# DeltaNet and low-rank mixer: 32x32 blocks moved by VectorE transpositions, norms from gram diagonals, and two products formed ahead of the recurrence

## The chip, the cores and the metric

One core of one Trainium2 chip runs the whole kernel in one launch. The metric is device time in microseconds, the median of several executions. Five engines work side by side, each with its own instruction queue: TensorE (PE, matmuls; its weight loads are listed as PEld), VectorE (DVE), ScalarE (ACT), GpSimd (POOL) and SyncE (SP, which here only issues DMAs).

## What is computed

Two parts follow each other. The first is a delta-rule attention over a sequence of 768 tokens, for 4 batches of 8 heads with 48 dimensions:

```python
k_n = k / (np.linalg.norm(k, axis=-1, keepdims=True) + 1e-06)
for t in range(S):
    y[:, :, t] = q_t @ state
    v_old = state^T k_t
    state = state + beta_t * outer(k_t, v_t - v_old)
```

The second is a mixer on the heads laid side by side (x is 4 x 768 x 384):

```python
u = x + ((x^T @ U) @ V)^T           # U: 768 x 32, V: 32 x 768
out = u + max(u @ w_ch1, 0) @ w_ch2 # 384 -> 1536 -> 384
```

The weights arrive as 64-bit floats and are turned into 32-bit ones on the chip.

## The kernel before

**Tiles.** The sequence is cut into 12 chunks of 64 tokens. Six chunks of one batch, all heads, are a unit; there are 8 units (n = 0 to 7, two per batch), and they alternate between two slots of SBUF. Four pairs of heads (j, r) fill the partitions.

**A unit's preparation.** `norms` squares k on ScalarE (L315), sums on VectorE (L318), takes root and reciprocal, multiplies with beta (L333), and turns the result on TensorE (L342) into `cp`. `grams` transposes k and q on TensorE (L367), copies them out (L370, L373), and forms K K^T and K Q^T (L382), copied out on ScalarE (L393) or masked on VectorE (L397). `blocks` needs the inverse of a unit lower triangular 64x64 matrix per head and chunk. It inverts the 32x32 diagonal blocks by forward substitution with one block per partition. So each block has to move from "rows on partitions" to "one block on one partition" and back. For unit 0 that is done by TensorE with an identity (L465, L522), for the others by DMAs through a scratch tensor in DRAM, issued from SP (L479 and L486 there, L544 and L549 back). The substitution is a chain of pairs of VectorE instructions (L497, L503): 31 pairs for a block of 32, or 15 pairs where the block is first split into two of 16 (`split == 2`, units 0 and 1), which are then joined by small matmuls (L579, L598). `joins` also combines the two 32-blocks into the 64-block (L621, L638), `diagonals` copies blocks on GpSimd (L658) and clears others (L664). The result is called zt below, the Z of the title.

**The recurrence** (`recur`) runs chunk after chunk through a batch: B = K S (L704), rhs = v - B on VectorE (L725), C = Z rhs (L734), a copy z on ScalarE (L743), the new state's product (L749), the state's sum on VectorE (L772). The output is q S (L715) plus a product with z (L759), copied to X by ScalarE (L685).

**The mixer.** `load_weights` brings 27 slices by GpSimd's DMA queue (L818) into two buffers, and converts each with five VectorE instructions (L834, L843, L849, L854, L862) and one on ScalarE (L839). `sums` adds slices of w_ch2 on GpSimd (L798), because the second layer is computed with 7 products in place of 8. `front` forms u and its transpose for 256 tokens (L885, L899, L903, L907, L910), `wide` the two layers for these 256 tokens: 72 matmul records of L972, then 84 of L1005, with GpSimd sums between them (L944, L951). There are 12 such steps, 3 per batch. A 32-bit matmul shows as two records.

**The order.** The program's order is made by a planner inside the kernel (`run`): every part is a generator that yields operations with an estimated cost, an engine, a PSUM buffer to take or give and keys to wait for, and each part has a place, the lower the sooner: recurrence of batch 0 at 1, the fronts at 2, preparation of units 0 and 1 at 10 and 14, weights at 21 to 40, recurrences of the other batches at 59, preparation of later units from 68, the wide steps at 95. The planner's result is the order on each engine's queue, and it is not changed at run time. PSUM has eight banks: three pairs (banks 0-1, 2-3, 6-7) and two single ones (4, 5); pair 6-7 is handed to `wide` when its first step begins.

Of the kernel before, what the change touches and what calls it, by code (L numbers as in the profile page):

```python
# [8 lines left out]
FP32 = mybir.dt.float32  # L9
# [6 lines left out]
L = 64  # L16
BK = 32
# [9 lines left out]
def kernel(  # L27
# [51 lines left out]
    BANK = dict(pair=[0, 2, 6], one=[4, 5], mix=[6, 7])  # L79
# [4 lines left out]
    state = dict(now=0.0, mode=None, hw=0.0, slow=1.9)  # L84
    free = dict(pair={0: 0.0, 1: 0.0, 2: 0.0}, one={0: 0.0, 1: 0.0}, mix={})
    done, parts, waits, ready, last = {}, {}, {}, {}, {}
    LAT = dict(pe=0.22, dve=0.06, act=0.06, pool=0.1, sp=0.0)
    SWITCH, HOLD = 0.15, 0.15

# [6 lines left out]
    def op(engine, cost, mode=None, take=None, give=(), lat=None, rush=False):  # L96
        return dict(e=engine, cost=cost, mode=mode, take=take, give=give,
                    rush=rush or bool(give), lat=LAT[engine] if lat is None else lat)
# [7 lines left out]
    def landing(packets, each=0.015):  # L106
        state["hw"] = max(state["hw"], state["now"]) + packets * each / 16
        return max(1.9, state["hw"] + 1.4 - state["now"])
# [16 lines left out]
    def run():  # L125
        while waits:
# [23 lines left out]
            for e, them in some.items():  # L150
                soon = min(at for at, _ in them)
                them.sort(key=lambda x: (not waits[x[1]]["rush"], x[1]))
                for at, i in them:
                    hold = HOLD if i[0] < 90 else SWITCH
                    if at > soon + hold:
                        continue
                    if not any(a < at and a + waits[x]["cost"] < at + 0.05 for a, x in them):
                        picks.append((at, i))
                        break
# [6 lines left out]
            cost = s["cost"] * (state["slow"] if s["mode"] in ("F", "Q", "T") else 1.0)  # L166
# [11 lines left out]
    def one(x):  # L178
        return P[:, BANK["one"][x]]

# [23 lines left out]
    def views(slot):  # L204
# [6 lines left out]
        ksq = slot[:, 6144 : 6144 + CS * D].rearrange("p (c s d) -> p c s d", c=UC, s=4)  # L211
        kz = slot[:, 9216 : 9216 + 2 * UC * D].rearrange("p (c j d) -> p c j d", c=UC, j=2)
        return kn, kq, pg, qk, qn, vn, ksq, kz

    units = [views(slots[n % 2]) for n in range(N)]
    for i in range(2):
        nc.vector.memset(units[i][0][:, :, :, D:DP], 0.0)
        nc.vector.memset(units[i][4][:, :, :, D:DP], 0.0)

    upper_rows = const.tile([128, 1], FP32, name="upper_rows")  # L220
    nc.vector.memset(upper_rows, 0.0)
    for i in range(4):
        nc.vector.memset(upper_rows[quarter(i, SB)], -1.0)
    bias_e = const.tile([128, 1], FP32, name="bias_e")
# [6 lines left out]
    nc.vector.memset(P[:, 0:4], 0.0)  # L231
    nc.vector.memset(P[:, 4:8], 0.0)
    nc.vector.memset(gs, 0.0)
    cts = [const.tile([128, BK], FP32, name=f"ct{i}") for i in range(2)]
    for t in cts:
        nc.vector.memset(t, 0.0)
    betas = const.tile([128, B, NC, 4], FP32, name="betas")
# [8 lines left out]
    clock["dve"], clock["pool"] = 8.0, 2.5  # L246
# [4 lines left out]
    def load(n, name, halves):  # L251
# [3 lines left out]
        yield need(("rec", n - 2))  # L255
# [9 lines left out]
        for g in halves:  # L265
# [10 lines left out]
            emitted((name, n, g), after)  # L276
# [4 lines left out]
    def load_beta():  # L281
# [3 lines left out]
        for g in range(2):  # L285
            yield op("pool", 0.6)
            nc.gpsimd.dma_start(out=beta_sb[:, g], in_=beta[:, 4 * g : 4 * g + 4])
        yield op("pool", 0.0, lat=landing(64, 0.1))
        for u in range(NU):
            x = yield op("pe", 0.6, "Q", take="one")  # L290
            p_bt = one(x)[:, 0 : 4 * B * UC].rearrange("p (c x) -> p c x", c=UC)
            for cu in range(UC):
                c = UC * u + cu
                for g in range(2):
                    nc.tensor.matmul(
                        p_bt[half(g), cu], beta_sb[:, g, c * L : c * L + L],
                        ident[0 : 4 * B, 0 : 4 * B], start=True, stop=True,
                    )
            yield op("dve", dve(4 * B * UC), give=[("one", x)])
            nc.vector.tensor_copy(  # L300
                out=betas[:, :, UC * u : UC * u + UC].rearrange("p b c s -> p c b s"),
                in_=p_bt.rearrange("p c (b s) -> p c b s", s=4),
            )
            emitted(("betas", u), 0.1)
            yield need(("gram", u))

    def landed(name, n):
        return need(*[(name, n, g) for g in range(2)])

    def norms(n):  # L310
        kn, _, _, _, _, vn, ksq, _ = units[n]
        b, hf = divmod(n, NU)
        yield landed("k", n)
        yield op("act", act(CS * D))
        nc.scalar.square(ksq, kn[:, :, :, 0:D])  # L315
        yield op("dve", dve(CS * D))
        norm = small.tile([128, UC, 4], FP32, name="norm", bufs=3)
        nc.vector.tensor_reduce(out=norm, in_=ksq, axis=AX.X, op=ALU.add)  # L318
        emitted(("ksq", n), 0.1)
        yield op("act", 0.2)  # L320
        norm_k, norm = norm, small.tile([128, UC, 4], FP32, name="norm_v", bufs=3)
        nc.scalar.sqrt(
            norm.rearrange("p c (r j) -> p c j r", r=2),
            norm_k.rearrange("p c (j r) -> p c j r", r=2),
        )
        yield need(("betas", hf))
        yield op("dve", 1.1)
        nc.vector.tensor_scalar_add(norm, norm, 1e-6)
        rec = small.tile([128, UC, 4], FP32, name="rec")
        nc.vector.reciprocal(rec, norm)  # L330
        nc.vector.tensor_tensor(out=rec, in0=rec, in1=rec, op=ALU.mult)
        ct = cts[n % 2][:, 0:CS].rearrange("p (r c j) -> p r c j", r=2, c=UC)
        nc.vector.tensor_tensor(  # L333
            out=ct.rearrange("p r c j -> p c r j"),
            in0=rec.rearrange("p c (r j) -> p c r j", r=2),
            in1=betas[:, b, UC * hf : UC * hf + UC].rearrange("p c (j r) -> p c r j", r=2),
            op=ALU.mult,
        )
        x = yield op("pe", 0.1, "J", take="one")
        p_ct = one(x)[:, 0:BK]  # L340
        for i in range(4):
            nc.tensor.matmul(  # L342
                p_ct[quarter(i)],
                cts[n % 2][quarter(i)],
                ident[quarter(i), quarter(i)],
                start=True,
                stop=True,
            )
        yield op("act", act(BK), give=[("one", x)])
        nc.scalar.copy(cp[:, n % 2], p_ct)  # L350
        emitted(("c", n), 0.1)
# [3 lines left out]
            out=vn, in0=vn, in1=norm[:, :, :, None].to_broadcast([128, UC, 4, D]), op=ALU.mult  # L355
# [3 lines left out]
    def grams(n):  # L359
        kn, kq, pg, qk, qn, _, _, _ = units[n]  # L360

        def turn(t, c0, i):
            x = yield op("pe", 0.45, "F", take="one")
            p_t = one(x).rearrange("p (x j t) -> p x j t", x=2, j=2)
            for c in range(2):
                for j in range(2):
                    nc.tensor.transpose(p_t[:, c, j], t[:, c0 + c, 2 * j : 2 * j + 2].rearrange("p s d -> p (s d)"), ident)  # L367
            if n == 0 and i == 0:
                yield op("dve", dve(512), give=[("one", x)])
                nc.vector.tensor_copy(out=kq[:, c0 : c0 + 2, :, i], in_=p_t)  # L370
            else:
                yield op("act", act(512), give=[("one", x)])
                nc.scalar.copy(kq[:, c0 : c0 + 2, :, i], p_t)  # L373

        def products(c0, i):
            x = yield op("pe", 0.47, "Q", take="pair")
            p_g = pair(x)[:, :, 0:256].rearrange("p r (c j t) -> p r c j t", c=2, j=2)
            for c in range(2):
                for j in range(2):
                    for par, g in QUADS:  # L380
                        rows = half(par, D)
                        nc.tensor.matmul(  # L382
                            p_g[half(g ^ (par * i)), par, c, j],
                            kq[rows, c0 + c, j, 0, half(g)],
                            kq[rows, c0 + c, j, i, half(g)],
                            start=True,
                            stop=True,
                        )
            at = slice(c0, c0 + 2)
            to = pg[:, :, at].rearrange("p r c j t -> p r (c j t)")  # L390
            if i == 0:
                yield op("act", act(512), give=[("pair", x)])
                nc.scalar.copy(to, p_g.rearrange("p r c j t -> p r (c j t)"))  # L393
            else:
                for par in range(2):
                    yield op("dve", dve(256), give=[("pair", x)] if par else (), rush=True)
                    nc.vector.tensor_tensor(  # L397
                        out=qk[:, par, at].rearrange("p c j t -> p (c j) t"),
                        in0=p_g[:, par].rearrange("p c j t -> p (c j) t"),
                        in1=mask_u[:, None, :].to_broadcast([128, 4, L]),  # L400
                        op=ALU.mult,
                    )
            emitted(("product", n, c0, i), 0.1)

        for i, (name, t) in enumerate((("k", kn), ("q", qn))):
            for c0 in range(0, UC, 2):
                yield landed(name, n)
# [658 lines left out]
```

## Time and profile before

| | |
|---|---|
| median of 3 executions | 720.76 us (719.04 to 721.79) |
| profiled execution: its time / span | 725.51 us / 723.7 us |
| mean granted TensorE clock | 0.884 |
| TensorE busy | 637.3 us (88%), 10344 matmul records |
| VectorE busy | 377.1 us (52%), 925 instructions |
| ScalarE / GpSimd busy | 182.9 us / 215.0 us |
| scratch DMAs of the blocks | 4 kinds, 28 issues each, 96 KB each |

The span runs from the first instruction to the last, and 1.8 us lie around it. In the table by stretches used below, each row gives a stretch in us, its length, then busy time and number of instructions of PE, PEld, DVE, ACT and POOL, the granted clock of TensorE, the mean share of the DMA engines, and GB/s. In the timeline a row gives start and duration in us, engine, line, operation, out<-in, and in brackets the idle time before it with what ended it.

### The profile page before, as it was taken

The numbers are of one execution on the slowest core, as the hardware profiler recorded it, in microseconds if no ns is written. First come the engines' busy times: TensorE is split into PE (matmuls) and PEld (weight loads), VectorE is DVE, ScalarE is ACT, GpSimd is POOL, SyncE is SP. The second block draws the span as 40 slices with busy tenths as digits, with TensorE's granted clock in tenths as the row PEclk, the third lists the DMA queues.
The fourth block names the chain that finished last, engine by engine and source line by source line (L and its number), as shares of the span: only waits on it lengthen the run. The fifth ranks groups of instructions, "written<-read, shape, count | busy, mean of one in ns | idle before, by whom it ended". The sixth has DMA issues, their size and how long they took to land.

```text
span 723.7 us, 23375 instructions
## 1 busy us (share of the span) xinstructions
PE 637.3 (88%) x10344; PEld 540.5 (75%) x10344; DVE 377.1 (52%) x925; ACT 182.9 (25%) x399; POOL 215.0 (30%) x281
## 2 busy tenths in 40 slices
PE   5667688659598899999798999999799999999998
PEld 4556576528486688789686887798677887989997
DVE  7577768799958631249678240469494111201001
ACT  3232235325121241331112322421113112020110
POOL 7326341233450250130350511123604302231412
PEclk9965555559798999999979999999799799999999
DMA  9731439852060231342211321521402000000000
GB/s 155 126 92 28 120 84 184 183 125 67 0 122 24 45 73 36 74 88 56 54 36 34 74 56 39 109 48 36 90 24 45 3 24 2 23 0 23 1 23 22
DMA packets 132964, 44.27 MB, mean 61 GB/s; under 512 B 126336, under 2 KB 129408, under 8 KB 132864
## 3 DMA queue, kind: packets, MB, share of 16 engines
q1 hardware_dynamic: 127776, 30.20, 21.2%
q0 software_dynamic: 3488, 12.29, 6.5%
q8 instruction: 81, 1.33, 0.8%
q10 hardware_dynamic: 1600, 0.30, 0.3%
q14 instruction: 19, 0.16, 0.1%
HBM read 32.54 MB, written 10.22 MB: 59 GB/s over the span
## 4 chain that ended last, share of the span: by engine, by line
PE 52%; DVE 29%; DMA 8%; issue 4%; SPq 3%; ACT 1%; POOL 1%; ACTq 0%; DVEq 0%; POOLq 0%
PE P L1005 18%; PE P L972 16%; DVE prod L497 11%; DVE xt L503 10%; PE P L638 2%; PE P L621 2%; SPq L269 2%; PE P L382 2%; DMA slot<-in_q_dram 2%; PE P L899 2%; PE P L367 2%; PE P L734 2%; DMA scr<-xt 2%; DMA wide<-in_moe_w_ch_dram 1%; PE P L704 1%
## 5 line engine op out<-in xcount | busy, mean ns | idle before, releaser
L972 PE MATMUL P<-ut,w_sb 128*128 128x256 f32 x864 | 213.3, 396 | 0.0
L972 PEld LDWEIGHTS P<-ut,w_sb 128*128 128x128 f32 x864 | 161.8, 194 | 24.8 <-issue 0.6
L1005 PE MATMUL P<-w_sb,hs 128*128 128x192 f32 x720 | 129.5, 333 | 0.0
L1005 PEld LDWEIGHTS P<-w_sb,hs 128*128 128x128 f32 x720 | 118.3, 192 | 3.2
L944 POOL TENSOR_TENSOR S<-hs 128x384 f32<-128x384 f32 x24 | 24.7, 1030 | 256.6 <-ACT hs L928 256.6
L957 DVE TENSOR_TENSOR X<-X,P 128x192 f32<-128x192 f32 x84 | 29.5, 351 | 133.4 <-PE P L1005 133.2
L497 DVE TENSOR_TENSOR prod<-gs,xt 128x112 f32<-128x112 f32 (+21 forms) x216 | 86.6, 401 | 6.0
L503 DVE TENSOR_TENSOR xt<-xt,prod 128x112 f32<-128x112 f32 (+21 forms) x216 | 84.2, 390 | 8.0 <-DVE prod L497 0.7
L928 ACT ACTIVATE hs<-P 128x512 f32<-128x512 f32 x72 | 43.0, 597 | 167.6 <-PE P L972 157.5
L1005 PE MATMUL P<-w_sb,S 128*128 128x192 f32 x288 | 56.5, 350 | 5.3 <-POOL S L944 5.3
L1005 PEld LDWEIGHTS P<-w_sb,S 128*128 128x128 f32 x288 | 50.6, 204 | 6.7 <-POOL S L944 5.8
L367 PE MATMUL P<-ident,slot 128*128 128x128 f32 x192 | 37.9, 331 | 9.1 <-DMA slot<-in_q_dram 7.7
L685 ACT COPY X<-P 64x192 f32<-64x192 f32 x96 | 30.1, 314 | 53.4 <-PE P L759 52.8
L658 POOL COPY slot<-zc 32x384 f32<-32x384 f32 x64 | 33.0, 516 | 27.4 <-DVE zc L606 21.3
L382 PE MATMUL P<-slot 48*64 48x64 f32 x1536 | 39.0, 250 | 2.4 <-DVE slot L397 0.7
L382 PEld LDWEIGHTS P<-slot 48*64 48x64 f32 x1536 | 32.6, 159 | 9.6 <-issue 3.4
L743 ACT COPY z<-P 128x192 f32<-128x192 f32 x48 | 15.2, 317 | 89.7 <-PE P L734 89.4
L367 PEld LDWEIGHTS P<-ident,slot 128*128 128x128 f32 x192 | 26.2, 166 | 13.7 <-issue 9.8
L772 DVE TENSOR_TENSOR s<-s,P 128x192 f32<-128x192 f32 x40 | 14.0, 349 | 40.7 <-PE P L749 40.3
L704 PEld LDWEIGHTS P<-s,slot 48*64 48x64 f32 x704 | 16.7, 155 | 24.7 <-DVE s L772 9.4
L734 PEld LDWEIGHTS P<-rhs,slot 64*64 64x64 f32 x704 | 16.9, 155 | 23.3 <-DVE rhs L725 13.1
L734 PE MATMUL P<-rhs,slot 64*64 64x48 f32 x704 | 22.6, 250 | 12.4 <-DVE rhs L725 12.4
(102 smaller groups left out, 769.9 us busy)
## 6 DMA issues: line engine op xcount, KB each, us to landing
wide<-in_moe_w_ch_dram POOLq DMA_DIRECT2D x24, 384.0 KB, 4.0
slot<-in_k_dram SPq DMA_DIRECT2D x84, 72.0 KB
slot<-in_q_dram SPq DMA_DIRECT2D x64, 72.0 KB
out_dram<-X SPq DMA_DIRECT2D x24, 192.0 KB
slot<-in_v_dram SPq DMA_DIRECT2D x48, 72.0 KB
scr<-slot SPq DMA_DIRECT2D x28, 96.0 KB
gs<-scr SPq DMA_DIRECT2D x28, 96.0 KB
scr<-xt SPq DMA_DIRECT2D x28, 96.0 KB
```

What stands on the lines that cost most here:

```text
L367: nc.tensor.transpose(p_t[:, c, j], t[:, c0 + c, 2 * j : 2 * j + 2].rearrange("p s d -> p (s d)"), ident)
L382: nc.tensor.matmul(p_g[half(g ^ (par * i)), par, c, j], kq[rows, c0 + c, j, 0, half(g)], kq[rows, c0 + c, j, i, half(g)], start=True, stop ...
L497: nc.vector.tensor_tensor(out=prod, in0=gb[:, :, j : j + 1, j + 1 :].to_broadcast([128, split, m, w]), in1=xb[:, :, 0:m, j : j + 1].to_bro ...
L503: nc.vector.tensor_tensor(out=xb[:, :, 0:m, j + 1 :], in0=xb[:, :, 0:m, j + 1 :], in1=prod, op=ALU.subtract,)
L658: nc.gpsimd.tensor_copy(out=heads(pg[quarter(i)])[:, at, a : a + BK], in_=zc[quarter(i), at])
L685: nc.scalar.copy(x[half(c % 2), c // 2, 4 * D * g : 4 * D * (g + 1)].rearrange("p (j r d) -> p r j d", r=2, d=D), states(p_y)[half(g)],)
L734: nc.tensor.matmul(states(p_c)[half(g ^ par), par, j], zt[half(g), par, cu, j], rhs[half(g), 2 * par + j], start=True, stop=True,)
L928: nc.scalar.activation(hs[:, fs[0] : fs[1] + 1 : fs[1] - fs[0]], p_f, ACTF.Relu)
L944: nc.gpsimd.tensor_tensor(out=to, in0=a, in1=c, op=how)
L957: nc.vector.tensor_tensor(out=to, in0=to, in1=p, op=ALU.add)
L972: nc.tensor.matmul(p_f[:, fs.index(f)], w1_sb[:, t, f * 128 : (f + 1) * 128], ut[:, t], start=(t == 0), stop=(t == KT - 1),)
L1005: nc.tensor.matmul(p_o, a[:, f], w2_sb[:, w, f], start=(first and f == 0), stop=(f == HF - 1), skip_group_check=True,)
```

## The change

1. **Moves.** The DMAs through DRAM and the matmuls with the identity that moved blocks are gone. ScalarE and VectorE gather the diagonal blocks in a tile `diag`, a VectorE transposition (in blocks of 32x32) brings them to one block per partition, and another brings the result back.
2. **Norms.** The squares and their sum are gone; the root is taken of the diagonal of the moved gram blocks. `cp` needs no turn on TensorE any more; the norms for v and the betas are turned by VectorE.
3. **Ahead of the recurrence.** `prepare` forms (Z K)^T and Z v, three chunks at a time. The recurrence then has B = (Z K) S, z = Z v - B on VectorE, the state's product and the sum; C and its ScalarE copy are gone. The outputs become parts of their own (`outputs`).
4. **Splits.** Units 2 and 3 are also split into blocks of 16.
5. **Bundles.** Transpositions and gram products come in blocks of one head pair over all six chunks (two for k, two for q). The joins of the 32-blocks are shared between upper and lower quarters.
6. **PSUM.** The single banks become a fourth pair; all small work takes pairs, of which three are left once `wide` has begun.
7. **Planner.** It counts TensorE's instruction words in lots of 256 and holds a lot back until 3.9 us after the last one; DMA landings are taken 1 us later than before. Two of the four last diagonal copies go to ScalarE, and loads wait until the outputs of the batch before are stored in X.

```diff
-    BANK = dict(pair=[0, 2, 6], one=[4, 5], mix=[6, 7])
+    BANK = dict(pair=[0, 2, 4, 6], mix=[6, 7])
+    LOT, FETCH = 256, 3.9
...
+            if s["e"] == "pe":
+                state["lot"] += s["words"]
+                if state["lot"] > LOT:
+                    state["lot"] -= LOT
+                    crossed = at + cost * (1 - state["lot"] / s["words"])
+                    late = max(0.0, state["fetched"] - crossed)
+                    cost += late
+                    state["fetched"] = crossed + late + FETCH
...
-        yield need(("rec", n - 2))
+        yield need(("rec", n - 2), *[("x", b - 1, UC * hf + c) for c in range(UC)])
...
-        nc.scalar.square(ksq, kn[:, :, :, 0:D])
-        nc.vector.tensor_reduce(out=norm, in_=ksq, axis=AX.X, op=ALU.add)
+        yield need(("laid", n), ("seeded", n))
+        nc.scalar.sqrt(norm, flat[:, 0 : BK * BK : BK + 1])
...
+        nc.vector.tensor_tensor(out=cp[:, n % 2], in0=rec, in1=betas[:, hf, b], op=ALU.mult)
+        nc.vector.tensor_copy(
+            out=xt.rearrange("p s t -> p (s t)")[:, 0 : BK * BK : BK + 1], in_=cp[:, n % 2]
+        )
+        nc.vector.transpose(rows, norm)
...
+                to = diag[:, 0:CS].rearrange("p (r c j) t -> p r c j t", r=2, c=UC)[:, :, :, j]
+                nc.scalar.mul(to, p_g[:, :, :, 0:BK], even[:, 0:1])
+                for r in range(2):
+                    nc.vector.scalar_tensor_tensor(
+                        out=to[:, r], in0=p_g[:, r, :, BK:L], scalar=even[:, 1:2], in1=to[:, r],
+                        op0=ALU.mult, op1=ALU.add,
+                    )
+                nc.scalar.copy(pg[:, :, :, j], p_g)
...
-        split = 2 if n < NU else 1
+        split = 2 if n in (0, 1, 2, 3) else 1
...
-            for i in range(4):
-                nc.sync.dma_start(out=gs[quarter(i, CS), 0:BK], in_=scr[i])
+        yield need(*[("diag", n, j) for j in range(2)], ("substituted", n - 1))
+        nc.vector.transpose(gs[:, 0:BK], diag.rearrange("p q t -> p t q"))
+        emitted(("laid", n))
...
+        nc.vector.transpose(
+            zz[:, 0 : BK * BK].rearrange("p (q t) -> p t q", t=BK),
+            xt[:, 0:BK].rearrange("p s t -> p t s"),
+        )
...
+        def prepare(n, h):
+            yield need(("joined", n), ("grams", n), ("scaled", n))
+            cs = range(3 * h, 3 * h + 3)
+            for c in range(3):
+                for j, par, g in heads:
+                    nc.tensor.matmul(
+                        p_k[half(par), g, c, j], kn[half(g), cs[c], 2 * j + par],
+                        zt[half(g), par, cs[c], j], start=True, stop=True,
+                    )
+            for c in range(3):
+                for j, par, g in heads:
+                    nc.tensor.matmul(
+                        p_v[half(g ^ par), par, c, j * D : j * D + D], zt[half(g), par, cs[c], j],
+                        vn[half(g), cs[c], 2 * par + j], start=True, stop=True,
+                    )
+            nc.scalar.copy(
+                kq[:, cs[0] : cs[2] + 1, :, 0].rearrange("p c j (g t) -> p (c j) g t", g=2),
+                p_k.rearrange("p g c j t -> p (c j) g t"),
+            )
+            nc.vector.tensor_copy(
+                out=vn[:, cs[0] : cs[2] + 1].rearrange("p c (r j) d -> p r c (j d)", r=2), in_=p_v,
+            )
...
-            xc = yield op("pe", 0.35, "Q", take="pair")
-            nc.scalar.copy(z.rearrange("p (r j) d -> p r (j d)", r=2), p_c)
+                yield need(("y", b, c - 3)) if c > 2 else []
+                z = zs[c] = small.tile([128, 4, D], FP32, name="z", bufs=3)
+                nc.vector.tensor_tensor(
+                    out=z.rearrange("p (r j) d -> p r (j d)", r=2),
+                    in0=vn[:, cu].rearrange("p (r j) d -> p r (j d)", r=2),
+                    in1=p_b, op=ALU.subtract,
+                )
...
+                yield need(("z", b, c), ("b", b, min(c + 1, NC - 1)))   # in outputs, ahead of the product with z
```

## The prediction

> **What bounds the kernel now.** I read the table by stretches first, to see where TensorE is short of work.
>
> ```profile
> 105.00:146.00 41.00, 29.07 (x731) 24.14 (x730) 32.26 (x76) 18.41 (x41) 9.28 (x16) 0.50 0.86 182
> 146.00:162.00 16.00, 8.36 (x43) 4.06 (x44) 15.20 (x30) 4.04 (x8) 6.68 (x7) 0.54 0.53 119
> 162.00:183.00 21.00, 21.00 (x190) 17.45 (x190) 20.28 (x42) 10.65 (x19) 6.62 (x7) 1.00 0.21 68
> 183.00:195.00 12.00, 2.99 (x13) 2.09 (x11) 11.59 (x17) 0.95 (x2) 7.71 (x6) 0.71 0.00 0
> 195.00:724.00 529.00, 504.34 (x6823) 430.57 (x6822) 225.31 (x581) 120.00 (x270) 138.11 (x165) 0.96 0.20 44
> ```
>
> Two stages differ. From 195 us on TensorE is busy 504.3 of 529 us: it is the bound, and only less work or fewer gaps (24.7 us idle, and (1 - 0.96) x 529 = 21 us of lowered clock) shorten it. Before 195 us it waits, at half clock, and in the rows from 146 us VectorE is full (15.2 of 16, 11.6 of 12). What starts the second stage shows in the timeline:
>
> ```profile
> 183.97 1.50 DVE L503 TENSOR_TENSOR xt<-xt,prod 128x252 f32<-128x252 f32 x1
> 190.06 1.56 POOL L798 TENSOR_TENSOR w_sb<-w_sb 128x576 f32<-128x576 f32 x1
> 193.66 1.54 PE L907 MATMUL P<-ident,X 128*128 128x128 f32 x6 [9.01 <-DVE X L903]
> ```
>
> The last weight slice is converted at 183.6, its last sum (L798) ends at 191.6, and L1005 starts at 195. The conversion is late because VectorE is also doing unit 2's unsplit substitution (L503). The third view is the timeline of one chunk of the first recurrence:
>
> ```profile
> 120.75 0.68 PE L704 MATMUL P<-s,slot 48*64 48x48 f32 x16
> 122.17 0.34 DVE L725 TENSOR_TENSOR rhs<-slot,P 128x192 f32<-128x192 f32 x1
> 122.57 0.68 PE L734 MATMUL P<-rhs,slot 64*64 64x48 f32 x16
> 123.36 0.32 ACT L743 COPY z<-P 128x192 f32<-128x192 f32 x1
> 125.89 0.35 DVE L772 TENSOR_TENSOR s<-s,P 128x192 f32<-128x192 f32 x1
> 126.38 0.68 PE L704 MATMUL P<-s,slot 48*64 48x48 f32 x16
> ```
>
> One chunk takes 126.38 - 120.75 = 5.6 us. Last, a drain in the second stage (another like it lies at 508 to 515 us):
>
> ```profile
> 355.92 1.01 PE L907 MATMUL P<-ident,X 128*128 128x128 f32 x6 [1.81 <-DVE X L903]
> 359.44 0.98 POOL L445 MEMSET xt<- 128x1056 f32 x1 [11.94 <-DMA scr<-xt]
> 362.50 2.29 PE L1005 MATMUL P<-w_sb,S 128*128 128x192 f32 x6 [2.65 <-POOL S L944]
> ```
>
> GpSimd stands 11.9 us in front of a memset until the scratch DMA has read xt, and the sums behind it on its queue hold up L1005.
>
> [...] clock 0.51 in 362 to 370 us, after the 2.65 us gap, and 0.50 in most of the first stage. [...] L558 does 384 columns in 562 ns. [...] L503 at 252 columns takes 0.42 us at 171 us and 1.50 us at 184 us beside L798.
>
> **The change part by part**, against the span of 723.7 us.
>
> *Start of the second stage.* VectorE is busy 140.8 us up to 183.6. L497 and L503 have 96 instructions and 40.2 us in it; units 0 and 1 own 60 of them at about 0.26 us (15.6 us), so some 24.6 us are unit 2's substitution, and 5.1 us more are unit 2's norms, masks and scaling (L318 1.35, six of L397 2.5, L490 1.23); neither is a condition for the weights. 111 us remain. Gone: two sums of squares L318 (2.7), copies L370 (2.1), PSUM memsets (3.5) and gs's (0.9) against 1.8 for the new one, and 12 masks of 0.417 become 8 of about 0.55 (-0.6): together -8. Added for two units: 8 gathers like L606 (0.42) = 3.4; 4 copies of 576 columns at about 0.75 = 3.0; small turns about 1; and 4 transpositions of 1024 columns. These no row shows. By L558, 1024/384 x 562 ns = 1.5 us; they are strided on one side, and strided L535 took 824 ns where straight L891 took 555 ns for 384 columns; 2.9 us is double L558's pace. They can't be free, since each replaces nothing on VectorE. I take 2.0, so 8 us. Sum: 111 - 8 + 15 = 118 us. At the share of now (140.8/183.6 = 0.77) that ends at 153 us; at 0.85, with fewer waits for moves, at 139. I take 150, plus the 8 us of sums as now: L1005 starts at about 158 in place of 195: **-37**. The recurrence must not be later than that: the C step and z's copy drop from the chunk; z is now formed where rhs was (122.17), so about 1.8 of 5.6 us go, 12 x 3.8 = 46 us. Before, it began at 66 us; with unit 0's 256 + 256 identity matmul records gone I expect 55 to 60, so x is complete at about 105. A front and the first 72 records of L972 (15.5 us) fit before 158. So what is late next is weights, not attention.
>
> *Work moved ahead.* In the 50 us that TensorE then lacks work, unit 2 can be prepared: L367 3.0, L382 3.75, joins 3.4 + 6.2, prepare about 4.5 = 21 us at full clock, and unit 3's k as well (some 5). Unit 2's L367 and L382 and unit 3's k, some 11 us, lay before 195 already, so the gain is 26 - 11: **-15**. It is 0 if the weights, which come sooner by place, leave VectorE no room, and -22 with all of unit 3's grams.
>
> *TensorE work in the second stage.* Z v costs what C cost (same shape and count). (Z K)^T is new: 16 records a chunk, 36 chunks; 16 of L734 take 0.375 us, 32 of L382 0.62 us, so 0.31 to 0.45, taken 0.375: +13.5. Inner joins of units 2 and 3: 768 records at L621's 1.55/96 = 16 ns: +12.4 [...]. L342: -1.2. A wide group of 6 takes 1.295 us in a run of 72 and 1.49 between small groups, so a switch costs 0.2 us: the chunk's three small groups become two (-7), the bundles save 4 switches a unit (-5), prepare and inner joins add some 25 (+5). Sum **+18** (10 to 26).
>
> *Gaps in the second stage.* The two drains hold 1.8 + 2.65 and 1.6 + 2.6 us, and the half clock after them (8 us at 0.51, 7 at 0.56, and the next 10 at 0.88 and 0.80) costs 3.9 + 3.1 + 3.2. With the scratch DMAs gone, the memset no longer waits for one, and SP's queue loses 112 issues that stood between loads and stores. That is 19 us; new waits (below) give some back: **-12** (-20 to +5).
>
> *Costed at nothing.* ScalarE, 25% busy: it loses L743 (15.2 us) and L315 (9.3), gets gathers and larger copies, hidden by TensorE; uncovered, a copy costs about 0.6 us a group in the first stage. GpSimd gets two memsets less waiting and half of one copy set less. On VectorE the first transposition waits for the gathers, and conversions and state sums queue behind it; the second stage has VectorE busy 225 of 529 us, which hides it; uncovered it would be some 2 us a unit. On TensorE prepare waits for GpSimd's scaling (L354, 2.1 us) with wide groups queued behind. The counting of lots changes order only.
>
> Sum: 723.7 - 37 - 15 + 18 - 12 = 677.7 span, 679.5 with the 1.8 us around it. The profiled execution was 725.51 against a median of 720.76, so times 0.9935: **675 us**.
>
> **The rivals.** *More gain (650 us):* VectorE at 0.85 and conversions in every gap; start at 148 (-47), all of unit 2 and some of unit 3 ahead (-22), +18, gaps -20: 652.7, median 650. For it speaks that the first stage then waits for little; against it two weight buffers, 10 slices in 41 us at the best (L834, 105 to 146 us).
> *The weights hold the start (707 us):* the cadence of those slices, not VectorE's total, decides, transpositions cost 2.9, and the start is 172 (-23), with -6, +20 and -5: 709.7, median 707. For it speaks DMA's 0.86 share in that stretch; against it that the last 7 slices needed 37 us only beside unit 2's substitution.
> *Slower (733 us):* the PSUM pairs. In the second stage two pairs and two single banks become three pairs, which recurrence, outputs, bundles, prepare and fronts share. The gains above net of the added work are 37 + 15 + 12 - 18 = 46 us. If each of a chunk's two groups waits for a bank, 36 x 2 = 72 waits, it decides from 0.64 us each; at 0.8 us, 57.6 us: 735.3, median 733. Against it: an eviction is 0.35 us (L725, L772), and the order allows for it. For it: waits of 2.4 us before L734 when VectorE is filled with pairs of L497.
> That the scratch moves stay is excluded by the diff.
>
> **How the numbers follow.** Forecast 0.61 (own range 655 to 695), more gain 0.18, weights hold 0.14, slower 0.07. The range 645 to 708 leaves out the slow case, half of the third and a quarter of the second, 0.18. Within 0.5% of 720.76 (about what a measurement of this kernel can tell from no change) I see 0.05, the upper part of the third case; slower 0.07, faster 0.88.
>
> **What would show it.** Right: L1005's first record near 158 us, last conversion near 150; chunks of the first recurrence under 4 us; no wait of the xt memset for a DMA; TensorE busy after that point about 18 us more for the same work. Wrong: transpositions of 1024 columns over 3 us, first L1005 after 175, or TensorE idle after it over 40 us, waiting for evictions.

## The result, and the profile after

The changed kernel takes **754.08 us** (median of 4, 749.14 to 755.80) against 721.27 us for the kernel before beside it: a ratio of 1.0439, 95% interval 1.0375 to 1.0504. It is slower; the forecast was 675 us. The profiled execution took 749.14 us, its span is 747.4 us, the mean clock 0.881. The trace of the changed kernel is of the fastest of these four executions and that of the kernel before of one (725.51 us) slower than its four, so the two spans lie 23.7 us apart, the medians 32.8.

Lines have moved: L972 is now L990, L1005 L1026, L862 L880, L798 L815, L903 L921, L907 L925, L497 and L503 are L490 and L496. L503 is now a transposition.

The table by stretches, of the kernel after (columns as before: stretch, length, then busy time of PE, PEld, DVE, ACT, POOL, clock, DMA share, GB/s):

```profile
105.00:146.00 41.00, 34.63 (x660) 28.09 (x653) 35.88 (x85) 22.84 (x42) 8.44 (x11) 0.92 0.63 145
146.00:200.50 54.50, 30.86 (x947) 26.11 (x945) 51.89 (x104) 10.98 (x22) 27.01 (x30) 0.61 0.12 38
200.50:300.00 99.50, 86.06 (x2022) 72.97 (x2017) 48.14 (x111) 28.36 (x59) 17.97 (x22) 0.94 0.25 48
300.00:400.00 100.00, 80.66 (x1917) 67.97 (x1916) 64.38 (x150) 26.74 (x59) 22.98 (x32) 0.93 0.15 32
400.00:500.00 100.00, 79.11 (x1484) 67.17 (x1483) 79.24 (x187) 23.02 (x47) 29.56 (x37) 0.88 0.13 26
500.00:747.40 247.40, 242.06 (x1795) 216.88 (x1793) 31.20 (x79) 37.02 (x72) 55.47 (x50) 1.00 0.04 14
200.50:747.40 546.90, 487.88 (x7212) 425.00 (x7206) 222.97 (x526) 115.15 (x234) 125.97 (x140) 0.95 0.12 26
```

The same stretches of the kernel before:

```profile
300.00:400.00 100.00, 93.25 (x1247) 79.35 (x1241) 68.87 (x175) 24.93 (x52) 27.29 (x31) 0.95 0.28 60
400.00:500.00 100.00, 99.54 (x1608) 83.94 (x1601) 44.66 (x103) 31.41 (x69) 25.28 (x29) 1.00 0.30 62
```

Two things are to be seen. The second stage starts at 200.5 us, not at 158, and VectorE is full right up to it (51.89 of 54.5 us). And where TensorE was nearly always busy before, it now stands: from 300 to 500 us it is idle for 40.2 of 200 us, against 7.2 before. From 500 us on it is busy again (242.06 of 247.4), with VectorE almost free. Over the whole span TensorE is busy 621.5 us, 16 less than before (637.3), and idle 747.4 - 621.5 = 125.9 us, 39.5 more than before (723.7 - 637.3 = 86.4); 34.3 of these 39.5 us lie in the second stage. **The loss is idle time of TensorE.**

What stands in front of the second stage, in the timeline of the kernel after:

```profile
189.16 0.56 DVE L880 SCALAR_TENSOR_TENSOR w_sb<-upper,power 128x384 f32<-128x384 f32 x1
189.86 4.31 POOL L815 TENSOR_TENSOR w_sb<-w_sb 128x576 f32<-128x576 f32 x3 [4.11 <-DVE w_sb L880]
191.44 1.47 DVE L490 TENSOR_TENSOR prod<-gs,xt 128x120 f32<-128x120 f32 x1
192.95 1.36 DVE L496 TENSOR_TENSOR xt<-xt,prod 128x120 f32<-128x120 f32 x1
194.34 0.29 DVE L490 TENSOR_TENSOR prod<-gs,xt 128x126 f32<-128x126 f32 x1
```

The last weight slice is converted at 189.7 us, its sums follow, and around them VectorE runs a substitution: of unit 3 (174.7 to 201.7 us), where it had been unit 2 in the kernel before. In 146 to 200 us the trace has 22.5 us of L490 and L496 of units 2 and 3 on VectorE, and 17 us of weight conversion.

And one gap of the second stage, on TensorE and VectorE, again in the timeline of the kernel after:

```profile
417.72 1.45 PE L917 MATMUL P<-tt,v_sb 128*128 128x384 f32 x4
418.62 1.24 DVE L490 TENSOR_TENSOR prod<-gs,xt 128x252 f32<-128x252 f32 x1
...
425.82 0.42 DVE L496 TENSOR_TENSOR xt<-xt,prod 128x247 f32<-128x247 f32 x1
426.15 1.01 DVE L921 TENSOR_TENSOR X<-X,P 128x384 f32<-128x384 f32 x2
426.84 0.45 PE L925 MATMUL P<-ident,X 128*128 128x128 f32 x1 [7.67 <-DVE X L921]
```

L917's product is ready at 419.2 us. L921 takes it out of PSUM (an eviction) within 1 us, but it comes up only at 426.15: in VectorE's queue twelve substitution instructions of unit 6 (418.62 to 425.82, most of them left out above) stand ahead of it. TensorE's next instruction needs L921's result, so it waits 7.67 us, with wide groups queued behind. That the planner had put L921 there because it expected VectorE to be further on is the theory tested below.

### The profile page after: what moved, and what is told of

Its sections match the earlier page's. It is cut to its first block, busy times and chain, and to the rows that moved or that the text cites. A ratio compares the mean times of both kernels' runs of the same rounds, so it can differ in the third digit from the quotient of the medians.

```text
span 747.4 us, 25030 instructions
## 1 busy us (share of the span) xinstructions
PE 621.5 (83%) x11304; PEld 539.9 (72%) x11304; DVE 396.9 (53%) x928; ACT 183.5 (25%) x369; POOL 208.9 (28%) x265
## 3 DMA queue, kind: packets, MB, share of 16 engines
q1 hardware_dynamic: 81856, 19.18, 13.5%
## 4 chain that ended last, share of the span: by engine, by line
PE 42%; DVE 20%; issue 2%; ACT 2%; DVEq 0%
PE P L990 18%; PE P L1026 17%; DVE prod L490 6%; DVE xt L496 6%; DVE zz L503 1%; PE P L917 1%; DVE slot L431 1%; PE P L781 1%; PE P L753 1%; PE P L925 1%; DVE gs L481 1%; DVE z L766 1%; ACT X L652 1%; DVE slot L420 1%; DVE X L921 1%
## 5 line engine op out<-in xcount | busy, mean ns | idle before, releaser
L990 PE MATMUL P<-ut,w_sb 128*128 128x256 f32 x864 | 205.2, 391 | 3.6 <-ACT hs L946 3.6
L990 PEld LDWEIGHTS P<-ut,w_sb 128*128 128x128 f32 x864 | 163.3, 194 | 26.7 <-ACT hs L946 4.0
L1026 PE MATMUL P<-w_sb,hs 128*128 128x192 f32 x720 | 128.2, 335 | 0.5 <-DVE X L975 0.5
L1026 PEld LDWEIGHTS P<-w_sb,hs 128*128 128x128 f32 x720 | 120.5, 195 | 3.8 <-issue 1.2
L490 DVE TENSOR_TENSOR prod<-gs,xt 128x30 f32<-128x30 f32 (+20 forms) x184 | 77.5, 421 | 4.4
L496 DVE TENSOR_TENSOR xt<-xt,prod 128x30 f32<-128x30 f32 (+20 forms) x184 | 73.0, 397 | 6.3
L1026 PE MATMUL P<-w_sb,S 128*128 128x192 f32 x288 | 51.7, 336 | 0.0
L1026 PEld LDWEIGHTS P<-w_sb,S 128*128 128x128 f32 x288 | 48.7, 196 | 0.5
L407 PE MATMUL P<-slot 48*64 48x64 f32 x1536 | 36.6, 260 | 10.9 <-DVE slot L613 6.3
L407 PEld LDWEIGHTS P<-slot 48*64 48x64 f32 x1536 | 32.9, 171 | 15.3 <-DVE slot L613 6.4
L380 PE MATMUL P<-ident,slot 128*128 128x128 f32 x192 | 31.9, 315 | 11.0 <-DMA slot<-in_k_dram 7.0
L921 DVE TENSOR_TENSOR X<-X,P 128x384 f32<-128x384 f32 x24 | 12.7, 547 | 46.5 <-PE P L917 46.1
L624 POOL COPY slot<-zz 32x384 f32<-32x384 f32 x48 | 24.6, 512 | 40.1 <-DVE zz L559 38.2
L380 PEld LDWEIGHTS P<-ident,slot 128*128 128x128 f32 x192 | 25.0, 160 | 14.7 <-issue 13.5
L969 POOL TENSOR_TENSOR hs<-hs,S 128x768 f32<-128x768 f32 x12 | 22.0, 1829 | 41.5 <-PE P L1026 41.5
L766 DVE TENSOR_TENSOR z<-slot,P 128x192 f32<-128x192 f32 x44 | 15.5, 353 | 31.1 <-PE P L753 30.0
L925 PE MATMUL P<-ident,X 128*128 128x128 f32 x72 | 13.5, 312 | 20.5 <-DVE X L921 20.3
L363 POOL TENSOR_TENSOR slot<-slot,norm_rows 128x1152 f32<-128x1152 f32 x8 | 18.8, 2349 | 40.2 <-DMA slot<-in_q_dram 28.1
```

The source lines that it names most:

```text
L380: nc.tensor.transpose(p_t[:, c // 3, c % 3], t[:, c, 2 * j : 2 * j + 2].rearrange("p s d -> p (s d)"), ident,)
L407: nc.tensor.matmul(p_g[half(g ^ (par * i)), par, c], kq[rows, c, j, 0, half(g)], kq[rows, c, j, i, half(g)], start=True, stop=True,)
L490: nc.vector.tensor_tensor(out=prod, in0=gb[:, :, j : j + 1, j + 1 :].to_broadcast([128, split, m, w]), in1=xb[:, :, 0:m, j : j + 1].to_bro ...
L496: nc.vector.tensor_tensor(out=xb[:, :, 0:m, j + 1 :], in0=xb[:, :, 0:m, j + 1 :], in1=prod, op=ALU.subtract,)
L624: nc.gpsimd.tensor_copy(out=to, in_=of)
L766: nc.vector.tensor_tensor(out=z.rearrange("p (r j) d -> p r (j d)", r=2), in0=vn[:, cu].rearrange("p (r j) d -> p r (j d)", r=2), in1=p_b, ...
```

## The experiments

**Theory:** TensorE's order is fixed; VectorE runs later than the planner thinks, so evictions and fronts that TensorE waits for sit behind substitutions, most of all in 260 to 500 us. **Rivals:** the late start; TensorE's added work; the planner's new lot and landing figures; the luck of one order, as an edit of the plan reorders all engines. "Idle" below is the span less TensorE's busy time over the whole span.

### What stands ahead of the weights

Hold back the substitution of units 2 and 3:

```diff
 def blocks(n):
...
+        if n in (2, 3):
+            yield need(("weights", 26))
         yield need(*[("diag", n, j) for j in range(2)], ("substituted", n - 1))
```

> The gathers' transposition and the substitution of units 2 and 3 may start only after the last weight slice. Theory (these two units' VectorE work stands ahead of the weights and sets the start of the second stage): last conversion at 150 to 165 us instead of 189, first L1026 at 160 to 175 instead of 200.5; the substitutions return later, so the time is 725 to 745. Rival (the weights' own loads set the pace): last conversion after 180 and the time within 8 us of 754.

Measured: 743.78 us, ratio 1.0289 (1.0231 to 1.0347). The stage after its first L1026 (L1028 here):

```profile
155.70:744.70 589.00, 512.86 (x8122) 445.37 (x8118) 271.65 (x641) 122.51 (x250) 143.35 (x160) 0.92 0.12 26
```

The time is within the theory's. The first record moves by 45 us, to 155.7, so these units did hold up the start (the last conversion, which ends at 168.8, still comes after it). But TensorE's work after it grows by 25.0 us (512.9 against 487.9), its idle time by 17.1 (76.1 against 59.0): the span gains 2.7 us, and the median 10.3. One reason shows right behind the first record:

```profile
168.74 1.92 DVE L483 STREAM_TRANSPOSE gs<-slot 128x1024 f32<-128x1024 f32 x1
181.58 0.35 DVE L977 TENSOR_TENSOR X<-X,P 128x192 f32<-128x192 f32 x1
182.07 0.66 PE L1028 MATMUL P<-w_sb,S 128*128 128x192 f32 x1 [12.60 <-DVE X L977]
```

As soon as the last slice is converted, VectorE turns to the held unit 2: transposition, norms, masks and the first pairs stand ahead of L977, which takes the first L1028 products out, and TensorE waits 12.60 us for it. With two waits for slices before it (2.61 and 4.81 us), TensorE is busy only 6.4 of the first 26.4 us. So this edit brings the first record 45 us ahead, but the steady work only to 182 us. What an early start is worth without such a wait behind it was not tried.

Split only units 0 and 1 (`split = 2 if n < NU else 1`):

> Only units 0 and 1 are split, as in the kernel before. Theory (VectorE's work of units 2 and 3 holds up the weights): their substitutions become some 12 us longer each, the first L1026 goes to 205 to 225, and 12 us of inner joins go: 750 to 770. Rival (added TensorE work is what costs): 738 to 745 with the start unchanged.

Measured: 746.17 us, ratio 1.0309 (1.0241 to 1.0377), start at 206.3 us. The start moved as the theory said, the time fell between theory and rival. TensorE's busy time falls to 606.3 us and its idle time rises to 138.2: most of what one gives, the other takes.

### The planner's figures

Lots, landing, hold and clock factor as in the kernel before (the changed planner also has a longer window for the parts of lowest place, and takes its factor for a lowered clock for all of TensorE's work; the list of the change leaves these two out):

```diff
-    LOT, FETCH = 256, 3.9
+    LOT, FETCH = 10 ** 9, 3.9
...
-        return max(2.0, state["hw"] + 2.4 - state["now"])
+        return max(1.9, state["hw"] + 1.4 - state["now"])
...
-                    hold = 0.7 if i[0] < 13 else HOLD if i[0] < 90 else SWITCH
+                    hold = HOLD if i[0] < 90 else SWITCH
...
-            cost = s["cost"] * (state["slow"] if s["mode"] else 1.0)
+            cost = s["cost"] * (state["slow"] if s["mode"] in ("F", "Q", "T") else 1.0)
```

> Lots not counted, and landing time, hold and clock factor of the planner as in the kernel before; everything computed is that of the changed kernel. Theory (units 2 and 3 stand ahead of the weights whatever the planner counts): 745 to 760, first L1026 after 190. Rival (the new planner figures, not the new operations, gave the order that costs): 690 to 725, with the first L1026 before 185 and less TensorE idle time after it.

Measured: 741.76 us, ratio 1.0246 (1.0180 to 1.0313), first L1026 at 209.9: the start is the theory's, the time is neither's.

Price the transpositions right (`dve(BK * BK)` becomes 2.0 at both):

> The planner prices the transpositions of 1024 columns at 2.0 us instead of 1.22; nothing else is changed. Theory (in the second stage VectorE runs later than the planner thinks, and TensorE's fixed order waits for it): idle time of TensorE after the first L1026 falls from 59 us by 10 or more, 735 to 748. Rival (the price of 16 instructions is too small a part of the lateness; what moves is only the order): within 8 us of 754, idle within 8 us of 59.

Measured: 739.57 us, ratio 1.0224 (1.0164 to 1.0283); idle after the first L1026 falls from 59.0 to 46.2. Time and idle are the theory's figures, but the run before it got an idle time of 45.8 by an unlike edit, so this proves nothing until it is known what order alone does.

### Work left out, order kept

Here the planner counts the instructions and only their issue is dropped, so every engine keeps the changed kernel's order. First the substitutions of units 4 to 7 (in the loop: `if n >= 4: continue` after the `yield`):

> The 62 substitution instructions of each of units 4 to 7 are not issued; the planner still counts them, so every engine's order is that of the changed kernel. The output of those units is therefore not the reference's. Theory (in 260 to 500 us TensorE's fixed order waits for evictions that sit in VectorE's queue behind these instructions): idle time of TensorE after the first L1026 falls from 59 us by 30 to 39, to 20 to 29, and the time is 712 to 724. Rival (TensorE's own small matmuls, their fetches and their order make the gaps): idle stays over 45 and the time over 738.

Measured: **712.21 us**, ratio 0.9843 (0.9769 to 0.9916). The stage after, and the place shown above (L923 and L927 are L921 and L925):

```profile
201.30:710.70 509.40, 482.97 (x7210) 421.90 (x7206) 125.32 (x278) 115.04 (x234) 124.60 (x140) 0.97 0.12 27
```

```profile
399.02 1.45 PE L919 MATMUL P<-tt,v_sb 128*128 128x384 f32 x4
399.94 1.13 DVE L923 TENSOR_TENSOR X<-X,P 128x384 f32<-128x384 f32 x2 [11.04 <-PE P L919]
400.64 1.03 PE L927 MATMUL P<-ident,X 128*128 128x128 f32 x6 [0.16 <-DVE X L923]
```

VectorE now waits for TensorE (11.04 us) and L927 waits 0.16 us where it waited 7.67. Idle after the first L1026 (L1028 here) is 509.4 - 483.0 = 26.4 us, 32.6 less, with the same order and the same matmuls. By itself the run leaves one rival: TensorE could have waited for the substitution's result and not for what stands behind it in the queue. The trace of the kernel after settles this. Of TensorE's waits after the first L1026, VectorE ends 40.5 us, and only 3.0 us of these are waits for the substitution's own result (L581 and L584, for the tile zz into which it is turned back); the rest are mostly results of other work that VectorE takes out of PSUM. In this run VectorE ends 8.6 us. So the gaps are VectorE's queue. The 26.4 us left are about what the kernel before has (24.7).

The two transpositions of units 4 to 7 (`if n < 4:` ahead of each):

> The two transpositions of 1024 columns are not issued in units 4 to 7 (the output of those units is not the reference's); 8 instructions, 16 us of VectorE; the order of all else is that of the changed kernel. Theory (the whole of VectorE's queue counts): as leaving out 97 us of substitution took 32.6 us of TensorE's idle time, 16 us take some 5 to 10; 743 to 749. Rival (the transpositions stand alone on the path, joins and gathers wait for nothing else): 14 us or more, below 740.

Measured: 740.52 us, ratio 1.0235 (1.0168 to 1.0303), idle after the start 49.1. The idle time fell by 9.9 us, within the theory's figure; the median, 13.6 lower, is between theory and rival.

The (Z K)^T products of units 2 to 7 (`range(3 if n < 2 else 0)`):

> The (Z K)^T products of units 2 to 7 are not issued (their copies are; the output of those units is not the reference's); the order of all else is that of the changed kernel. 36 chunks at the 0.375 us of the forecast are 13.5 us, at the 23.1 us of L704 over 48 chunks 17. Theory (VectorE is the bound in 260 to 500 us, TensorE outside it): part of it only, 743 to 750. Rival (TensorE's added work is what costs): 13 us or more, below 741.

Measured: 744.63 us, ratio 1.0290 (1.0221 to 1.0358), in the theory's interval. The profile doesn't show the saving: with 576 records fewer TensorE is busy 622.5 us, but the clock of that execution is 0.859, where it was 0.881 in the kernel after and 0.878 to 0.882 in the three other executions of this run.

### What order alone does

`HOLD`, the planner's window for a preferred operation, is 0.18 instead of 0.15, in the changed kernel and in the kernel before, then 0.20 in both:

> The planner's window for a preferred instruction is 0.18 instead of 0.15 us; all operations are those of the changed kernel. It measures how far a mere change of order moves the time. Theory (the loss lies in the structure): within 8 us of 754. Rival (754 is an unlucky order): 740 to 745, as the runs so far gave for three unlike edits.

> The same edit in the kernel before. If 721 is a lucky order, it comes out at 728 to 740; if not, within 5 us of 721.

> The kernel before with a window of 0.20 us: a second sample of what order alone does to it. The first gave 732.6. Theory (order alone moves these kernels by some 10 us): 722 to 738.

> The changed kernel with a window of 0.20 us: a second sample of the same. The first gave 745.5. Theory: 738 to 756, above the kernel before with the same window by 8 us or more. Rival (the whole difference is luck of the order): within 5 us of it.

| window | kernel before | changed kernel |
|---|---|---|
| 0.15 | 721.27 (1) | 754.08, 1.0439 (1.0375 to 1.0504) |
| 0.18 | 732.64, 1.0127 (1.0056 to 1.0197) | 745.47, 1.0296 (1.0199 to 1.0392) |
| 0.20 | 731.87, 1.0103 (1.0049 to 1.0158) | 751.10, 1.0387 (1.0341 to 1.0434) |

Order alone moves either kernel by some 10 us. Of its three orders, 721 is the lucky one of its kernel, and 754 the unlucky one. The means are 728.6 and 750.2: by this estimate about 22 us of the 33 belong to the structure and the rest to luck. Three orders each are few, so the split is rough; but the two ranges, 721 to 733 and 745 to 754, do not meet. The first sample of the changed kernel lay at the edge between theory and rival, the other three where the theory had them. By this measure the runs on start, split, lots and price (740 to 746) tell little by their times alone.

### VectorE priced right, and given slack

Plan a pause between a unit's substitution and the next transposition:

```diff
-        emitted(("substituted", n))
+        emitted(("substituted", n), 12.0 if n >= 4 else 0.0)
```

> In units 4 to 7 the next unit's transposition is planned 12 us after the last substitution instead of at once. Theory (the wait for the scratch DMAs was, in the kernel before, the slack in which VectorE caught up with its plan): idle in 300 to 500 us falls from 40 us to 25 or less, 735 to 745. Rival (the sum of VectorE's work decides, not how it is spread): 748 to 758.

Measured: 731.60 us, ratio 1.0104 (1.0029 to 1.0180). Idle in 300 to 500 us is 20.6, as expected, and the gain is larger: 22.5 us.

To this pause, add prices: 2.0 us for the two transpositions, as above, and more for the substitutions. By the planner's own clock the substitutions of units 4 to 7 take 25.7, 26.4, 24.1 and 26.8 us; in the trace they take 32.1, 34.1, 35.6 and 30.4, 1.28 times as long (first to last instruction, with what lies between):

```diff
-            yield op("dve", 2 * dve(split * m * w) - 0.08)
+            yield op("dve", (1.3 if n >= 4 else 1.0) * (2 * dve(split * m * w) - 0.08))
```

> Slack as before, transpositions priced at 2.0 us, and the substitutions of units 4 to 7 at 1.3 times the planner's price (33 us of a measured substitution for 26 planned). Theory (TensorE waits because VectorE is later than planned): idle in 300 to 500 us falls below the 20.6 us of the run with slack alone, to 12 or less, 715 to 728. Rival (slack was itself only another order): 732 to 748.

Measured: **721.58 us** (20 executions), ratio 0.9991 (0.9955 to 1.0027). The time is the theory's; idle in 300 to 500 us is 17.0, more than the 12 expected. The kernel with pause and both prices is called calibrated below. The same with a window of 0.18:

> The calibrated changed kernel (slack of 12 us, transpositions at 2.0, substitutions at 1.3 times) with a window of 0.18 us. Theory (the calibration works by its mechanism): 715 to 732, at least 13 us below the uncalibrated 745.5 with that window. Rival (721.6 was a lucky order): 736 to 748.

Measured: 733.74 us, ratio 1.0155 (1.0102 to 1.0208): 11.7 below its uncalibrated pair, just short of both figures of the theory, and below the rival's. The calibration holds under another order, less strongly. With either window the calibrated kernel is level with the kernel before (721.27 and 732.64). And the price of the substitutions in the kernel before:

> The kernel before, with its planner pricing the substitutions of units 4 to 7 at 1.3 times. Theory (the kernel before has slack between its substitutions already, from the scratch DMAs): within 6 us of 724. Rival (any kernel of this planner gains when VectorE is priced right, so the comparison with the calibrated changed kernel was unfair): 705 to 716.

Measured: 725.17 us, ratio 1.0024 (0.9996 to 1.0051), as the theory had it: against the kernel before as it stands it gains nothing. But that one is a lucky order; against the two others (732.64 and 731.87) it would be a gain of 7 us, so a small gain is not excluded.

Hold and slack together, then hold with slack and prices from unit 2 on:

> Both edits: substitution of units 2 and 3 after the weights, and 12 us planned between substitution and next transposition in units 4 to 7. Theory (an earlier start alone moves work from before it to after it; what counts is the sum of TensorE's idle time): first L1026 at 155 to 165, TensorE busy after it about 25 us more than in the run with slack alone, and the time within 8 us of that run's 731.6. Rival (the 45 us of the start are worth their full time once VectorE has slack): below 710.

> Units 2 and 3 after the weights, with the calibrated prices and the slack of 12 us from unit 2 on. The start comes out near 155 us again. Theory (an early start only moves VectorE's and TensorE's work behind it): within 12 us of the calibrated 721.6 and 733.7, so 712 to 742. Rival (the late start costs its time once the order is calibrated): below 705.

Measured: 746.30 us, ratio 1.0297 (1.0243 to 1.0351), and 724.46 us, 1.0021 (0.9994 to 1.0048). The first missed both figures: slack did not help that order. It has the same 12.60 us wait for L977 as the run with hold alone; that the low price of units 2 and 3 is the rest of the reason is not shown. The second is the theory's. Its stage after the first L1028, at 157.6 us:

```profile
157.60:722.40 564.80, 505.22 (x8126) 439.37 (x8118) 282.13 (x642) 123.41 (x251) 143.99 (x162) 0.94 0.12 28
```

Calibrated, but with the planner's older lot and landing figures:

> The calibrated changed kernel with lots, landing, hold and clock factor of the planner as in the kernel before. Theory (what counts is VectorE's price and slack; lots and landing only reorder): 715 to 737. Rival (lots and landing help once VectorE is priced right): 740 to 755.

Measured: 723.47 us, ratio 1.0025 (1.0003 to 1.0048), with the first L1026 at 219.0 us. So calibrated orders whose second stage begins at 157.6, 208.0 and 219.0 us end within 3 us of one another, less than order alone moves them: neither the first record nor lots and landing decide. The early one again has a wait behind its start, 10.33 us with L977 behind unit 2's work, and 4.39 and 4.40 us for slices; its steady work begins at 184 us. No order tried, of those that compute everything, beats the kernel before clear of noise.

## Why the prediction was wrong

**Right.** The transpositions cost 1.94 and 2.03 us, taken at 2.0:

```profile
L503 DVE STREAM_TRANSPOSE zz<-xt 128x1024 f32<-128x1024 f32 x8 | 16.2, 2031 | 0.3
L481 DVE STREAM_TRANSPOSE gs<-slot 128x1024 f32<-128x1024 f32 x8 | 15.5, 1940 | 0.2
```

An undisturbed chunk of the first recurrence (B to B, L753 at 66.43 and 76.81 us, three chunks) takes 3.5 us, taken at 3.8. No memset of xt waits for a DMA any more. The PSUM rival did not come: the longest wait for a bank that I can name in the kernel after is 6.25 us, once (L407 for L613), against the 46 us in all from which it would decide, and there too the late instruction was VectorE's. That the time came out slow, as this rival has it, is by another mechanism.

**The sum, by its three parts** (us; the forecast's are the start at 158, TensorE's work 504.3 - 15 + 18, and idle 24.7 - 12):

| | forecast | kernel after | hold, calibrated | calibrated |
|---|---|---|---|---|
| first L1026 | 158 | 200.5 | 157.6 | 208.0 |
| TensorE busy after it | 507.3 | 487.9 | 505.2 | 479.5 |
| TensorE idle after it | 12.7 | 59.0 | 59.6 | 34.5 |
| sum (span; the forecast's is 677.7 but for rounding) | 678.0 | 747.4 | 722.4 | 722.0 |

**First failed step: "Start of the second stage", -37.** "Neither is a condition for the weights" is true, and with units 2 and 3 held back the first record comes at 157.6, the forecast at 158. But the plan left them ahead. I had taken a condition for an order: VectorE works in the order of the plan, and whatever the planner fits in while a slice is under way stands before the next one. I had even counted that work as a gain, "work moved ahead -15", without leaving its VectorE part in the 118 us. (A reading of this step is off too: up to 183.6 us unit 2's substitution takes 20.6 us and not 24.6, as units 0 and 1 take 0.30 us an instruction and not 0.26.) The late start does not cost its full length. Much of what is not done after it is done before it, as the table's first two rows show: +42.5 and -19.4, together 23.1 of the 69.4 us that the sum is off. And no run got these back by an earlier first record.

**Second failed step: "Gaps in the second stage", -12, and with it "Costed at nothing".** This is the larger part of the miss: +46.3 us in the kernel after. (The +46.9 with hold and calibration is another mixture: 19 us of it are the three waits behind the early first record, told above.) "The second stage has VectorE busy 225 of 529 us, which hides it" was an average over the stage. VectorE's work lies bunched: 143.6 of 200 us in 300 to 500, and 31 of 247 after that. From the first to the last substitution of units 4 to 7, in the kernel before and in the kernel after:

```profile
325.80:548.70 222.90, 209.39 (x3048) 177.51 (x3046) 138.71 (x360) 53.99 (x119) 58.48 (x73) 0.95 0.25 53
276.20:479.30 203.10, 158.75 (x3250) 135.60 (x3242) 159.21 (x376) 51.86 (x104) 49.10 (x59) 0.91 0.19 37
```

VectorE goes from 62% busy to 78%, and TensorE's idle time from 13.5 us to 44.3: 30.8 of the 34.3 us of the second stage lie here. In a bunch, what TensorE needs next is behind what VectorE does now. The run without the substitutions of units 4 to 7 gave back 32.6 of the 46.3 us. The two drains by DMA did go; the waits on VectorE that took their place are larger.

**Why the kernel before bears it.** There a unit's blocks were away by DMA before and after its substitution, and other evictions could run in that time. The traces show this slack from the last substitution instruction of unit 4 to the first of unit 5, in the kernel before, in the kernel after, and with the planned pause:

```profile
355.40:368.90 13.50, 10.34 (x194) 9.45 (x196) 4.09 (x10) 2.16 (x5) 9.05 (x13) 0.75 0.63 120
308.30:317.50 9.20, 5.68 (x272) 4.87 (x274) 8.53 (x12) 3.36 (x8) 5.75 (x10) 0.70 0.02 4
310.70:330.10 19.40, 16.18 (x480) 13.26 (x479) 11.91 (x19) 6.89 (x14) 10.57 (x15) 0.82 0.01 3
```

VectorE is free for 9.4, 0.7 and 7.5 us there, and between units 6 and 7 for 8.9, 0.6 and 7.5. That this slack is why the kernel before bears its substitutions is likely: giving it back in the plan gained 22.5 us. A run that takes it from the kernel before was not made.

**TensorE's work, +18 and -15,** agrees as a sum to 2 us (505.2 against 507.3, in the run whose start is the forecast's), but at least in part by luck: in that run unit 2's joins and its products of Z all come after the start, where the -15 had them before it. The parts were not separated. Leaving out most of (Z K)^T saved 9.5 us of the median, where +13.5 were forecast for it, but that run does not say how much of it was hidden.

**What stays open:** how fast a calibrated order with an early start would be. In the one tried, TensorE is busy only 109.8 of 142.4 us in 157.6 to 300; after its first record it still waits for the last slices, the last of which is converted at 172.5 us, and then for L977. So the first record of L1026 is a flattering mark, and my step took it for the start of the stage. An order with L977 ahead of unit 2's work would show what the start is worth. Also open is how much of the 11 us between the two kernels that the estimate above puts down to luck is luck.

## What to carry to other kernels

Where the order is fixed ahead of time, a busy share of 40% on a helper engine is no cover; look at the stretches in which its work is bunched, and at what stands in its queue ahead of the instruction that the main engine waits for. Taking a slow transfer out can also take out the pause in which the helper caught up, so price its instructions from the trace and plan the pause back in. An earlier first record of a stage is no earlier stage: see what TensorE waits for right behind it. And before an ordered program is compared with another, perturb both: here a change of 0.03 us in one planner constant moved either kernel by 9 to 11 us.

## What the runs showed of the hardware

The same VectorE instruction took 0.18 us at one place and 1.99 us beside a TENSOR_TENSOR of GpSimd. In the timeline of the kernel after:

```profile
448.01 2.95 POOL L363 TENSOR_TENSOR slot<-slot,norm_rows 128x1152 f32<-128x1152 f32 x1 [0.58 <-POOL slot L624]
449.01 1.99 DVE L490 TENSOR_TENSOR prod<-gs,xt 128x31 f32<-128x31 f32 x1
451.02 0.88 POOL L631 MEMSET slot<- 32x384 f32 x2
451.04 0.19 DVE L496 TENSOR_TENSOR xt<-xt,prod 128x31 f32<-128x31 f32 x1
```

L490 on 31 columns, 0.18 us elsewhere (at 276.19 us), takes 1.99 us and ends 0.04 us after GpSimd's instruction. A price by columns misses such times, and they are part of why a substitution planned for 26 us takes 33: of the 248 substitution instructions of units 4 to 7, 19 take over 1.3 times the shortest of their shape. Each of the 19 overlaps a TENSOR_TENSOR of GpSimd, as only 5 of the other 229 do, which all began before it. Together the 19 take 18.9 us more than the shortest would, of the 29 us by which these substitutions outlast their plan. That GpSimd's instructions are the cause is likely from this; by what means was not shown.
